# Layer norm and two-matmul MLP on one core: the third token tile loaded behind two weight pieces, its cells run later, and tile 3's chain rearranged

## The chip, the cores and the metric

The kernel runs on one core of a Trainium2 chip. A core has five engines with queues of their own: TensorE (PE, matmuls; its weight loads are listed as PEld), VectorE (DVE), ScalarE (ACT), GpSimd (POOL) and SyncE (SP, which here only issues transfers). Sixteen DMA engines carry the transfers. The metric is the device time of one execution in microseconds (us), as a median of several runs.

## The reference

```python
def reference(x, w1, b1, w2, b2):
    y = _layernorm(x, axis=-1)
    h = _gelu(jnp.einsum("bsd,df->bsf", y, w1) + b1)
    return jnp.einsum("bsf,fd->bsd", h, w2) + b2
```

x is 1 x 2048 x 1024, w1 is 1024 x 3584, w2 is 3584 x 1024, all bf16. The layer norm has no scale and no shift: (x - m) / sqrt(v + eps) for each token.

## The kernel before

The 2048 tokens are worked on in four blocks of 512, a block in four tiles of 128 tokens. Per block there are two matmul stages. The first (mm1) makes 28 rows r of 128 hidden channels: for each row, eight steps dt over the 1024 input channels, w1's piece as the weights and the transposed tokens (yT_sb) as the moving side, summed in one bank of PSUM (the accumulation memory, eight banks of 2 KB per partition). ACT reads the bank, applies gelu with the bias and writes hT_sb. The second (mm2) makes, for each of the four tiles, two halves of 512 output channels over 28 steps; DVE adds b2 (line 459) and SP stores.

Each of the five engines has a list of instructions in a fixed order, written out by hand for the start and, for DVE's later work, by a small planner (lines 631 to 646) from estimated times. Instructions wait on each other by semaphores; an engine that waits holds up all that is behind it in its list.

The change is in the start, block 0. There the transposed tokens are needed before the layer norm's statistics can be ready, so tiles 0, 1 and 2 (RAW) go through mm1 **raw**, unnormalised, and are corrected later:

- PE transposes a tile by eight matmuls against an identity (`pe_T`, line 335) into PSUM, one 128 x 128 block per input step dt. ACT copies the blocks into yT_sb (line 351). GROUPS_0 = (0, 4, 8) says that tiles 0 and 1 leave in two copies of four blocks; tile 2, by GROUPS_2 = (0, 2, 8), in two and six. Four banks take the groups: tile 0 in "t" and "2_0", tile 1 in "2_1" and "1_4", and tile 2 again in "t" and "2_0", so its transposes wait until ACT has read tile 0's.
- The **wave** is the first eight rows of mm1 (one bank each) on the three raw tiles. One matmul of it, one row r with one step dt, is a cell here (`wave_cell`, `pe_wave`, line 396). Its moving side is 128 columns per tile, with two columns of ones ahead of tile 0 that give the column sums of the weights.
- w1's first eight rows come in nine pieces, loads "w0" to "w8", in the order of PIECES: w0 holds dt 0 of rows 0 to 3, w1 (the load) dt 1, w2 dt 2 and 3, w3 dt 4 and 5, w4 dt 6 and 7, and w5 to w8 the same for rows 4 to 7, two steps each. (So "w0" to "w8" are pieces of the matrix w1.) w0 and w1 are 128 KB, the others, and a tile of x, 256 KB. SP issues them in the order of SP_FIRST_LOADS.
- For piece 0 the cells run for tiles 0 and 1 together (258 columns) and then for tile 2 (128); from piece 1 on, all three tiles at once (386).
- DVE takes the statistics (bn_stats, line 247, bn_aggr, line 257), POOL the power -0.5 (line 254). The means and the reciprocal deviations of the raw tiles are turned from columns into rows by DVE (`ops_row_turn`, line 479: turn_m for the means, turn_r for the deviations, four instructions each) and spread to all partitions by ACT (`put_row_spread`, line 485).
- **Tile 3** is normalised on DVE (line 261), transposed there within blocks of 32 (xq, line 489), and its sixteen pieces are moved into place by DVE (`moves_3`, line 494, those in DVE_MOVES) and ACT (`put_moves_3`, line 503, the rest). Its cells (line 396, 128 columns) follow the wave.
- DVE then corrects each bank of the wave (`ops_fix`, lines 532 and 535) and subtracts the means in yT_sb (`ops_centre`, line 525) for the rows of block 0 that follow; these are scaled at line 422.

DVE's order in the start is one line (542):

```python
seq = st[0] + st[1] + st[2] + turn_m + st[3] + turn_r[:3] + nm[3] + moves_3() + turn_r[3:] + ctr[:2]
```

and PE's order is that of the calls from line 546 on:

```python
pe_T(0, GROUPS_0, ("t", "2_0"))
pe_T(1, GROUPS_0, ("2_1", "1_4"))
pe_T(2, GROUPS_2, ("t", "2_0"))
```

with the wave's cells behind them.

Of the kernel before, what the change touches and what calls it, by code (L numbers as in the profile page):

```python
# [9 lines left out]
I32 = mybir.dt.int32  # L10

LN_EPS = 1e-5
P = 128
TB = 512
TPB = TB // P
# [4 lines left out]
TAIL_PIECES = (448, 64)  # L20
RAW = (0, 1, 2)
N_WARM = 25
GROUPS_0 = (0, 4, 8)
GROUPS_2 = (0, 2, 8)
HALVES = (0, 4, 8)
PIECES = ((0, 1, (0, 1, 2, 3)), (1, 2, (0, 1, 2, 3)), (2, 4, (0, 1, 2, 3)), (4, 6, (0, 1, 2, 3)), (6, 8, (0, 1, 2, 3)),
          (0, 2, (4, 5, 6, 7)), (2, 4, (4, 5, 6, 7)), (4, 6, (4, 5, 6, 7)), (6, 8, (4, 5, 6, 7)))
CENTRE = (0, 2, 4, 6, 8)
DVE_MOVES = ((0, 0), (1, 1), (2, 2), (3, 3), (0, 1), (1, 2), (2, 3))
W1_COLS = (512, 1024, 1024)  # L30
N_W2_CHUNKS = 4
SP_FIRST_LOADS = ("b1", "x0", "x1", "x2", "w0", "w1", "w2", "w3", "x3", "w4", "w5", "w6", "w7", "w8")
N_ONES = 2
PAD = 64

# [56 lines left out]
def bass_standalone__mixer_channel_mlp__prompt_kernel(  # L92
# [13 lines left out]
    DT = D // P  # L106
# [7 lines left out]
    R = R_WAVE  # L114
    assert R == NB1 + NB2 + 1 and R < FT
    assert NB1 + NB2 + 1 <= 8 and NB2 == 2
    assert all(c[-1] == DT for c in (GROUPS_0, GROUPS_2, HALVES))
    assert TPB == 4 and RAW == (0, 1, 2)
# [23 lines left out]
    with ExitStack() as es:  # L142
# [6 lines left out]
        yT_sb = sb("yT_sb", [P, 2, DT, PAD + TB], BF16)  # L149
# [26 lines left out]
        act = _Prog("s_act")  # L176
# [34 lines left out]
        def issue(item):  # L211
            if item == "b1":
                dma_q[0] = act
                dma(b1r_sb[:, :], b1.rearrange("(t p) -> t p", p=P), "b1", F * 2)
                dma_q[0] = sp
            elif item[0] == "x":
                load_x_tile(int(item[1:]))
            elif item[0] == "w" and int(item[1:]) < len(w1_chunks):
                load_w1(int(item[1:]))

        act.op(lambda e: e.preload_act_table(ACT.Gelu_apprx_tanh))
        for item in SP_FIRST_LOADS:
            issue(item)
# [8 lines left out]
        for b in range(2, NB):  # L232
# [4 lines left out]
                sig="ident")  # L237
# [7 lines left out]
        def op_stats(i, h):  # L245
            pw = D // parts(i)
            return (lambda e, i=i, h=h, pw=pw: e.bn_stats(st_sb[i][:, 6 * h:6 * (h + 1)],  # L247
                                                          x_sb[:, i, h * pw:(h + 1) * pw]),
                    [x_ev[i][h if len(x_ev[i]) == parts(i) else 0]], f"st{i}_{h}", 0.03 + pw * 0.0012)
# [41 lines left out]
        ybuf = lambda b: (b + 1) % 2  # L291
# [16 lines left out]
        def dve_put(o):  # L308
            dve.op(o[0], waits=o[1], sig=o[2])

        pe_t = [T_PE_START]
        bank_read = {}
        bank_of = {"t": ps_t[:, 0, :], "2_0": ps_2b[:, 0, :], "2_1": ps_2b[:, 1, :], "1_1": ps_1b[:, 1, :], "1_2": ps_1b[:, 2, :], "1_3": ps_1b[:, 3, :],
                   "1_4": ps_1b[:, 4, :]}
        ycol = lambda i: PAD + (i % TPB) * P
        raw_at = TB - len(RAW) * P
        one0 = raw_at - N_ONES

        def pe_T(i, groups, banks):
            blk = i // TPB  # L320
            src_ev = y_ev[i] if i in y_ev else [x_ev[i][0]] * DT
            evs = yT_ev.setdefault(i, [None] * DT)
            prev = None
            for k, (g0, g1) in enumerate(zip(groups[:-1], groups[1:])):
                bname = banks[k]
                for j in range(g0, g1):
                    waits = []
                    if bname != prev:
                        waits = ["ident"] + ([bank_read[bname]] if bname in bank_read else [])
                        off = 0  # L330
                    prev = bname
                    if j == g0 or src_ev[j] != src_ev[j - 1]:
                        waits.append(src_ev[j])
                    last = j == g1 - 1 and (k + 1 == len(banks) or banks[k + 1] != bname)
                    pe.op(lambda e, i=i, j=j, o=off, bap=bank_of[bname]: e.transpose(  # L335
                        out=bap[:, o:o + P], in_=x_sb[:, i, j * P:(j + 1) * P], identity=ident[:, :]),
                        waits=waits, sig=(f"tp{i}_{k}" if last else None))
                    evs[j] = f"te{i}_{k}"
                    off += P
            off = 0  # L340
            prev = None
            for k, (g0, g1) in enumerate(zip(groups[:-1], groups[1:])):
                bname = banks[k]
                if bname != prev:
                    off = 0
                prev = bname
                done = max(m for m in range(len(banks)) if banks[m] == bname)
                src = bank_of[bname][:, off:off + (g1 - g0) * P].bitcast(I32)
                src = src.rearrange("p (j s) -> p j s", j=g1 - g0)
                dst = yT_sb[:, 0 if i in RAW else ybuf(blk), g0:g1, ycol(i):ycol(i) + P].bitcast(I32)  # L350
                act.op(lambda e, dst=dst, src=src: e.copy(out=dst, in_=src), waits=[f"tp{i}_{done}"],  # L351
                       sig=f"te{i}_{k}")
                off += (g1 - g0) * P
                bank_read[bname] = f"te{i}_{k}"
            pe_t[0] += DT * 0.056

        unit_n = [0]
        bank_gelu = {}
# [124 lines left out]
        def put_row_spread(k, q0, q1):  # L483
            for q in range(q0, q1):
                act.op(lambda e, q=q: e.copy(out=row_b(k)[32 * q:32 * (q + 1)], in_=row_b(k)[0:32]),  # L485
                       waits=[f"row_q{k}"], sig=(f"row_{k}" if q == 3 else None))

        def moves_3():
            res = [(lambda e: e.transpose(out=xq_sb[:, :], in_=x_sb[:, 3, :]), [y_ev[3][-1]], "xq", 1.07)]
            for n, (tq, q) in enumerate([(tq, q) for tq in range(4) for q in range(4)]):  # L490
                src = xq_sb[32 * tq:32 * (tq + 1), :].rearrange("p (j q s) -> p j q s", j=DT, q=4)[:, :, q, :].bitcast(I32)
                dst = yT_sb[32 * q:32 * (q + 1), ybuf(0), :, ycol(3) + 32 * tq:ycol(3) + 32 * (tq + 1)].bitcast(I32)
                if (tq, q) in DVE_MOVES:
                    res.append((lambda e, src=src, dst=dst: e.tensor_copy(out=dst, in_=src), ["xq"],
                                ("tc3" if len(res) == len(DVE_MOVES) else None), 0.2))
            return res

        def put_moves_3():
            todo = [(tq, q) for tq in range(4) for q in range(4) if (tq, q) not in DVE_MOVES]
            for tq, q in todo:  # L500
                src = xq_sb[32 * tq:32 * (tq + 1), :].rearrange("p (j q s) -> p j q s", j=DT, q=4)[:, :, q, :].bitcast(I32)
                dst = yT_sb[32 * q:32 * (q + 1), ybuf(0), :, ycol(3) + 32 * tq:ycol(3) + 32 * (tq + 1)].bitcast(I32)
                act.op(lambda e, src=src, dst=dst: e.copy(out=dst, in_=src), waits=["xq"],
                       sig=("te3" if (tq, q) == todo[-1] else None))
            yT_ev[3] = ["te3"] * DT
# [32 lines left out]
        st = {i: [op_stats(i, 0), op_stats(i, 1), op_aggr(i)] for i in range(TPB)}  # L538
        nm = {3: ops_norm(3)}
        turn_m, turn_r = ops_row_turn(0), ops_row_turn(1)  # L540
        ctr = ops_centre()
        seq = st[0] + st[1] + st[2] + turn_m + st[3] + turn_r[:3] + nm[3] + moves_3() + turn_r[3:] + ctr[:2]
        for o in seq:
            dve_put(o)

        pe_b1()
        put_b1()
        pe_T(0, GROUPS_0, ("t", "2_0"))
        pe_T(1, GROUPS_0, ("2_1", "1_4"))
        pe_T(2, GROUPS_2, ("t", "2_0"))  # L550
        put_row_spread(0, 1, 4)
        wave = [new_unit() for _ in range(R)]
        opened = set()

        def wave_cell(r, dt, tiles, sig=None):
            waits = [] if r in opened else wave[r][1]
            opened.add(r)
            pe_wave(r, dt, tiles, wave[r][0], waits, sig)

        first = [(r, dt) for r in PIECES[0][2] for dt in range(*PIECES[0][:2])]  # L560
        for tiles in (RAW[:2], RAW[2:]):
            for r, dt in first:
                wave_cell(r, dt, tiles)
        cells = [(r, dt) for j0, j1, rows in PIECES[1:] for r in rows if r < R for dt in range(j0, j1)]
        for n, (r, dt) in enumerate(cells):
            wave_cell(r, dt, RAW, f"raw_{r}" if dt == DT - 1 else None)
        cs_ev = {}
# [34 lines left out]
        for b in range(NB):  # L602
            if b + 1 < NB:
                tiles = list(range((b + 1) * TPB, (b + 2) * TPB))
# [9 lines left out]
            for st in range(TPB):  # L614
                for dh in range(DH):
                    c0, c1 = dh * NCH, (dh + 1) * NCH
                    ob = (b * TPB + st) % NOB
                    prev = store_last.get((ob, dh))
# [14 lines left out]
        while ci < len(crit) or fi < len(fill):  # L633
            take_crit = fi >= len(fill)
            if not take_crit and ci < len(crit):
                rel_f, _, blk_f = fill[fi]
                if crit[ci][0] <= max(t_dve, rel_f) + CRIT_SLACK and blk_f > crit[ci][2]:
                    take_crit = True
            if take_crit:
                rdy, o, _ = crit[ci]  # L640
                ci += 1
            else:
                rdy, o, _ = fill[fi]
# [46 lines left out]
```

## Time and profile before

| | |
|---|---|
| time, median of 3 runs | 396.66 us (396.55 to 396.83) |
| the profiled execution | 396.68 us, of which the span, from the first to the last instruction, 395.3 us |
| mm1's matmuls (line 381, both banks' rows) | 152.4 and 31.9 us busy |
| mm2's matmuls (line 448) | 193.3 us busy |
| the start's cells (line 396, ps) | 13.1 us busy |
| ACT's gelu (line 406) | 64.0 and 12.4 us busy |
| DVE's transposes of the later blocks (line 303) | 83.7 us busy |
| HBM read, written | 19.14 MB, 4.19 MB |

In the views a row has the start and the length in us (in a timeline), or the busy time and the mean length in ns (in the groups), then the engine, the line of the kernel, the operation, what it writes <- what it reads, and the shapes. A bracket says how long the engine stood idle before the row and what released it. Rows of one kind that follow each other are merged, with their number behind the x; the length is then from the first one's start to the last one's end. The length of a PE row includes the time that a matmul needs to run through the array, so queued matmuls overlap: it is the distance between starts that says how fast they go. Transfers have the time from issue to landing.

### The profile page before, as it was taken

To read this page: it belongs to the slowest core of one execution; us is meant where nothing else is said; L and a number is where in the kernel's file an instruction comes from. 1 tells how busy PE (TensorE), PEld (TensorE's weight loads), DVE (VectorE), ACT (ScalarE), POOL (GpSimd) and SP (SyncE) were. 2 spreads that over 40 slices of the span, in tenths; PEclk is the share of its full clock that TensorE was granted. 3 is DMA by queue.
4 is the path that set the end of the run, shared out by engine and by line. 5 is a ranking of instruction groups with operands and counts; after the bars stand their busy time and mean duration, and the time that the engine had idled before them with its cause. 6 is when DMAs were issued, how large, how long until landed. Compare 5 with 4: busy or idle time off the path is not lost.

```text
span 395.3 us, 4518 instructions
## 1 busy us (share of the span) xinstructions
PE 390.3 (99%) x1904; PEld 184.5 (47%) x1938; DVE 162.8 (41%) x342; ACT 85.9 (22%) x139; POOL 10.5 (3%) x55
## 2 busy tenths in 40 slices
PE   8999999999999999999999999999999999999998
PEld 6744444444444444444444444444444444444444
DVE  6998889998999306987100000011100000001011
ACT  4655420000134332000023443000003334400000
POOL 3001000011001100000000000000000000000000
DMA  8999930000000000000000000000000000000000
GB/s 272 372 386 387 387 141 27 15 27 14 28 0 0 2 0 0 29 26 13 28 13 0 2 0 2 13 13 28 25 14 15 0 0 2 0 15 27 13 28 27
DMA packets 16077, 23.62 MB, mean 60 GB/s; under 512 B 1082, under 2 KB 8250, under 8 KB 16058
## 3 DMA queue, kind: packets, MB, share of 16 engines
q1 hardware_dynamic: 16016, 23.33, 16.7%
q8 instruction: 15, 0.25, 0.3%
q14 instruction: 4, 0.03, 0.0%
q10 hardware_dynamic: 42, 0.01, 0.0%
HBM read 19.14 MB, written 4.19 MB: 59 GB/s over the span
## 4 chain that ended last, share of the span: by engine, by line
PE 99%; issue 0%; ACT 0%; DVE 0%
PE ps L448 49%; PE ps L381 38%; PE ps_t L381 7%; PE ps L396 3%; PE ps L470 1%; PE ps_t L396 0%; ACT yT_sb L351 0%; PE ps_t L335 0%; PE ps L335 0%; DVE o_sb L459 0%; PE ps L508 0%
## 5 line engine op out<-in xcount | busy, mean ns | idle before, releaser
L448 PE MATMUL ps<-w_sb,hT_sb 128*128 128x512 bf16 (+2 forms) x909 | 193.3, 372 | 0.8
L381 PE MATMUL ps<-yT_sb,w_sb 128*128 128x512 bf16 x678 | 152.4, 379 | 0.9
L448 PEld LDWEIGHTS ps<-w_sb,hT_sb 128*128 128x128 bf16 x924 | 88.6, 98 | 105.2
L406 ACT ACTIVATE hT_sb<-ps,b_sb 128x512 bf16<-128x512 f32 x94 | 64.0, 687 | 234.7 <-PE ps L381 217.2
L381 PEld LDWEIGHTS ps<-yT_sb,w_sb 128*128 128x128 bf16 x696 | 68.1, 98 | 81.9
L459 DVE TENSOR_TENSOR o_sb<-ps,b_sb 128x512 bf16<-128x512 f32 (+2 forms) x33 | 22.3, 676 | 198.7 <-PE ps L448 198.5
L303 DVE STREAM_TRANSPOSE yT_sb<-x_sb 32x256 bf16<-32x256 bf16 x192 | 83.7, 436 | 21.9 <-PE ps_t L381 18.8
L381 PE MATMUL ps_t<-yT_sb,w_sb 128*128 128x512 bf16 x135 | 31.9, 379 | 0.1
L247 DVE BATCH_NORM_STATS2 st_sb<-x_sb 128x6 f32<-128x512 bf16 x32 | 21.0, 672 | 3.6 <-DMA x_sb<-in_x_dram 3.5
L381 PEld LDWEIGHTS ps_t<-yT_sb,w_sb 128*128 128x128 bf16 x136 | 13.3, 98 | 16.0
L406 ACT ACTIVATE hT_sb<-ps_t,b_sb 128x512 bf16<-128x512 f32 x18 | 12.4, 687 | 17.1 <-PE ps_t L381 14.6
L396 PE MATMUL ps<-yT_sb,w_sb 128*128 128x128 bf16 (+2 forms) x116 | 13.1, 269 | 0.0
L396 PEld LDWEIGHTS ps<-yT_sb,w_sb 128*128 128x128 bf16 x116 | 8.9, 98 | 3.5
L422 DVE TENSOR_TENSOR ps<-ps,row_r 128x384 f32<-128x384 f32 x17 | 9.2, 563 | 3.1 <-PE ps L381 2.8
L254 POOL TENSOR_TENSOR rstd_sb<-mv_sb,nhalf 128x1 f32<-128x1 f32 x13 | 7.1, 548 | 116.7 <-DVE mv_sb L257 116.7
L261 DVE TENSOR_SCALAR x_sb<-x_sb,mv_sb,rstd_sb 128x1024 bf16<-128x1024 bf16 x13 | 7.0, 541 | 1.9 <-POOL rstd_sb L254 1.3
L532 DVE SCALAR_TENSOR_TENSOR ps<-row_r,ncs,ps 128x384 f32<-128x384 f32 x7 | 4.2, 614 | 0.4 <-PE ps L396 0.4
L535 DVE TENSOR_TENSOR ps<-ps,row_r 128x384 f32<-128x384 f32 x7 | 3.9, 563 | 0.2
L525 DVE TENSOR_TENSOR yT_sb<-yT_sb,row_r 128x768 bf16<-128x768 bf16 x4 | 3.6, 952 | 0.0
L470 PE MATMUL ps<-const-bfloat16-1.0 128*128 128x128 bf16 x25 | 2.8, 309 | 0.8 <-PEq L675 0.8
L485 ACT COPY row_r<-row_r 32x384 f32<-32x384 f32 x6 | 3.1, 510 | 2.2 <-DVE row_r L479 2.1
L257 DVE BATCH_NORM_AGGREGATE mv_sb<-st_sb 128x2 f32<-128x15 f32 x13 | 2.9, 222 | 0.4
(33 smaller groups left out, 31.1 us busy)
## 6 DMA issues: line engine op xcount, KB each, us to landing
w_sb<-in_w_dram SPq DMA_DIRECT2D x4, 1792.0 KB, 18.3
w_sb<-in_w_dram SPq DMA_DIRECT2D x2, 2048.0 KB, 16.2
out_dram<-o_sb SPq DMA_DIRECT2D x31, 128.0 KB, 1.7
x_sb<-in_x_dram SPq DMA_DIRECT2D x3, 1024.0 KB, 14.4
w_sb<-in_w_dram SPq DMA_DIRECT2D x7, 256.0 KB, 4.9
x_sb<-in_x_dram SPq DMA_DIRECT2D x4, 256.0 KB, 3.4
w_sb<-in_w_dram SPq DMA_DIRECT2D x1, 1024.0 KB, 9.5
w_sb<-in_w_dram SPq DMA_DIRECT2D x2, 128.0 KB, 3.8
```

The lines of the kernel that those rows point to most:

```text
L247: return (lambda e, i=i, h=h, pw=pw: e.bn_stats(st_sb[i][:, 6 * h:6 * (h + 1)], x_sb[:, i, h * pw:(h + 1) * pw]), [x_ev[i][h if len(x_ev[i ...
L254: pool.op(lambda e, i=i, dst=dst, mv=mv: e.tensor_tensor(out=dst, in0=mv[:, 1:2], in1=nhalf[:, i:i + 1], op=ALU.pow), waits=[f"mv{i}", "nh ...
L261: return (lambda e, i=i, c0=c0, c1=c1: e.tensor_scalar(out=x_sb[:, i, c0:c1], in0=x_sb[:, i, c0:c1], scalar1=mv_sb[:, i, 0:1], scalar2=rst ...
L303: res.append((lambda e, src=src, dst=dst: e.transpose(out=dst, in_=src), waits, (f"tr{i}" if lastop else None), 0.47))
L381: pe.op(lambda e, b=b, r=r, dt=dt, bank=bank: e.matmul(unit_bank(bank)[:, 0:TB], lhsT=w1_sb[:, dt, r * P:(r + 1) * P], rhs=yT_sb[:, ybuf(b ...
L396: pe.op(lambda e: e.matmul(unit_bank(bank)[:, n0:n1], lhsT=w1_sb[:, dt, r * P:(r + 1) * P], rhs=yT_sb[:, 0 if tiles[0] in RAW else ybuf(0) ...
L406: act.op(lambda e, r=r, n0=n0, n1=n1, bank=bank: e.activation(out=hT_sb[:, r, n0:n1], in_=unit_bank(bank)[:, n0:n1], func=ACT.Gelu_apprx_tanh,
L422: crit.append((est[sig], (lambda e, reg=reg: e.tensor_tensor(out=reg, in0=reg, in1=row_b(1), op=ALU.mult), [sig, "row_1"], ready, 0.57), 0))
L448: pe.op(lambda e, sl=sl, ft=ft, c0=c0, c1=c1, bank=bank: e.matmul(ps_2[:, bank, 0:c1 - c0], lhsT=hT_sb[:, ft, sl * P:(sl + 1) * P], rhs=w2 ...
L459: crit.append((est[sig], (lambda e, ob=ob, c0=c0, c1=c1, bank=bank: e.tensor_tensor(out=o_sb[:, ob, c0:c1], in0=ps_2[:, bank, 0:c1 - c0], ...
L470: pe.op(lambda e: e.matmul(ps_1[:, 0, 0:P], lhsT=ones, rhs=ones, start=True, stop=True))
L532: return [(lambda e: e.scalar_tensor_tensor(out=reg, in0=row_b(0), scalar=ncs[:, c:c + 1], in1=reg, op0=ALU.mult, op1=ALU.add), [f"m1_0_{r ...
```

## The change

- SP's order of first loads puts x2 behind w0 and w1.
- GROUPS_0 becomes (0, 2, 8): tiles 0 and 1 leave PSUM in copies of two and six blocks. The copies, which `pe_T` put on ACT's list itself, get a function of their own, `put_copy`, and go in turn: tile 0's two blocks, tile 1's two blocks, tile 0's six, tile 1's six.
- The transposes of tile 2 and ACT's spread of the row of means are put behind the cells of pieces 0 and 1 for tiles 0 and 1. Piece 0's cells run for tile 0 and then for tile 1 alone; pieces 1 and 2 for tiles 0 and 1 together; tile 2's cells of pieces 0, 1 and 2 follow piece 2. From piece 3 on all three tiles run together as before.
- DVE does two of the four turns of the means before the statistics of tile 3 and two behind them; all four turns of the deviations go behind tile 3's moves. DVE does five of the sixteen moves, not seven; ACT eleven, not nine.

```diff
-GROUPS_0 = (0, 4, 8)
+GROUPS_0 = (0, 2, 8)
...
-DVE_MOVES = ((0, 0), (1, 1), (2, 2), (3, 3), (0, 1), (1, 2), (2, 3))
+DVE_MOVES = ((0, 0), (1, 1), (2, 2), (3, 3), (0, 1))
...
-SP_FIRST_LOADS = ("b1", "x0", "x1", "x2", "w0", "w1", "w2", "w3", "x3", "w4", "w5", "w6", "w7", "w8")
+N_EARLY = 2
+N_PAIR = 3
+SP_FIRST_LOADS = ("b1", "x0", "x1", "w0", "w1", "x2", "w2", "w3", "x3", "w4", "w5", "w6", "w7", "w8")
...
-        def pe_T(i, groups, banks):
+        def pe_T(i, groups, banks, copies=True):
...
+            pe_t[0] += DT * 0.056
+            for k in (range(len(banks)) if copies else ()):
+                put_copy(i, groups, banks, k)
+
+        def put_copy(i, groups, banks, k):
+            g0, g1 = groups[k:k + 2]
+            bname = banks[k]
...
+            act.op(lambda e, dst=dst, src=src: e.copy(out=dst, in_=src), waits=[f"tp{i}_{done}"],
+                   sig=f"te{i}_{k}")
+            bank_read[bname] = f"te{i}_{k}"
...
-        seq = st[0] + st[1] + st[2] + turn_m + st[3] + turn_r[:3] + nm[3] + moves_3() + turn_r[3:] + ctr[:2]
+        seq = st[0] + st[1] + st[2] + turn_m[:2] + st[3] + turn_m[2:] + nm[3] + moves_3() + turn_r + ctr[:2]
...
-        pe_T(0, GROUPS_0, ("t", "2_0"))
-        pe_T(1, GROUPS_0, ("2_1", "1_4"))
-        pe_T(2, GROUPS_2, ("t", "2_0"))
-        put_row_spread(0, 1, 4)
+        pe_T(0, GROUPS_0, ("t", "2_0"), False)
+        pe_T(1, GROUPS_0, ("2_1", "1_4"), False)
+        for k in range(2):
+            put_copy(0, GROUPS_0, ("t", "2_0"), k)
+            put_copy(1, GROUPS_0, ("2_1", "1_4"), k)
...
-        first = [(r, dt) for r in PIECES[0][2] for dt in range(*PIECES[0][:2])]
-        for tiles in (RAW[:2], RAW[2:]):
-            for r, dt in first:
-                wave_cell(r, dt, tiles)
-        cells = [(r, dt) for j0, j1, rows in PIECES[1:] for r in rows if r < R for dt in range(j0, j1)]
+        cells_of = lambda a, b: [(r, dt) for j0, j1, rows in PIECES[a:b] for r in rows for dt in range(j0, j1)]
+        for t in RAW[:2]:
+            for r, dt in cells_of(0, 1):
+                wave_cell(r, dt, (t,))
+        for r, dt in cells_of(1, N_EARLY):
+            wave_cell(r, dt, RAW[:2])
+        pe_T(2, GROUPS_2, ("t", "2_0"))
+        put_row_spread(0, 1, 4)
+        for r, dt in cells_of(N_EARLY, N_PAIR):
+            wave_cell(r, dt, RAW[:2])
+        for r, dt in cells_of(0, N_PAIR):
+            wave_cell(r, dt, RAW[2:])
+        cells = cells_of(N_PAIR, len(PIECES))
```

More of the change, by code (lines that the diff above doesn't have):

```diff
@@ L339, in pe_T @@
                     off += P
-            off = 0
[L341 to L355, printed above, removed]
+            pe_t[0] += DT * 0.056
[4 more added lines that the diff above has]
+            bname = banks[k]
+            assert banks.count(bname) == 1
+            off = 0
+            done = max(m for m in range(len(banks)) if banks[m] == bname)
+            src = bank_of[bname][:, off:off + (g1 - g0) * P].bitcast(I32)
+            src = src.rearrange("p (j s) -> p j s", j=g1 - g0)
+            dst = yT_sb[:, 0 if i in RAW else ybuf(i // TPB), g0:g1, ycol(i):ycol(i) + P].bitcast(I32)
+            act.op(lambda e, dst=dst, src=src: e.copy(out=dst, in_=src), waits=[f"tp{i}_{done}"],
+                   sig=f"te{i}_{k}")
+            bank_read[bname] = f"te{i}_{k}"
         unit_n = [0]
```

## The prediction

> **What bounds the kernel now.** I read the page first, then the chain of waits, then the timelines of PE and ACT over the first 25 us, then the landings of the first loads.
>
> ```profile
> span 395.3 us, 4518 instructions
> ...
> PE 390.3 (99%) x1904; PEld 184.5 (47%) x1938; DVE 162.8 (41%) x342; ACT 85.9 (22%) x139; POOL 10.5 (3%) x55
> ...
> PE 99%; issue 0%; ACT 0%; DVE 0%
> ```
>
> TensorE (PE) is the bound in all stages. So the change can only win where PE stands still, or by giving PE less to do. The timeline of PE from 4.98 us on shows the only place:
>
> ```profile
> 4.82 0.39 PE L335 MATMUL ps<-ident,x_sb 128*128 128x128 bf16 x4
> 5.78 0.27 PE L335 MATMUL ps_t<-ident,x_sb 128*128 128x128 bf16 x2 [0.58 <-ACT yT_sb L351]
> 5.89 0.50 PE L335 MATMUL ps<-ident,x_sb 128*128 128x128 bf16 x6
> 6.22 0.99 PE L396 MATMUL ps<-yT_sb,w_sb 128*128 128x258 bf16 x9
> ```
>
> The first line's four transposes start 0.056 us apart, so the array has taken the last at 4.82 + 4 x 0.056 = 5.04. Nothing starts until 5.78: **0.74 us of idle**. The view charges it to an ACT copy, but that copy was over at 4.73; the last to come is x2. Its transfer was issued at 1.69 and took 4.0 us, so it landed at 5.64, and PE's first transpose starts 0.14 after that. From 5.78 on matmul follows matmul at the pitch of its width (0.056 us for 128 columns, 0.110 for 258, 0.164 for 386, 0.216 for 512) up to 393.3. The single holes of 0.216 us, one per 50 matmuls, are missing records: the next matmul starts exactly two pitches later.
>
> **Ceiling.** The change splits 16 cells (a cell is one weight load with its matmul) in two: 4 of 258 columns, 12 of 386. The widths add up the same, and 2 x 0.056 - 0.110 and 0.110 + 0.056 - 0.164 are both 0.002 to 0.003, so this costs 16 x 0.0026 = 0.04 us. If all idle goes, the gain is 0.74 - 0.04 = 0.70 us, or 0.18%.
>
> **Loads.** SP issues one load every 0.47 us, whatever its order. From 2.5 us on the profile by stretches has the DMA engines full (share 0.85 to 1.16, 260 to 401 GB/s), so the order decides who waits, not the sum. A load counts as landed when the slowest of 16 engines has landed. In the trace, median engine and slowest:
>
> x0 3.37 and 3.50; x1 4.02 and 4.13; x2 4.67 and 5.64; w0 5.10 and 6.03; w1 5.50 and 6.37; w2 6.29 and 7.07; w3 7.05 and 7.74; x3 7.86 and 8.46.
>
> One engine falls 0.97 behind during x2 and stays 0.6 to 0.9 behind; over the eleven loads from x2 to w8 its middle lag is 0.70. After the change w0 and w1 (128 KB each) take the place of x2 (256 KB). By medians: w0 4.02 + 0.43 = 4.45, w1 4.85, x2 5.5, and **w2 as now, 6.27, since the same bytes lie ahead of it**. Slowest engine with 0.70 of lag: w0 about 5.2, w1 5.5, x2 6.2, w2 6.97. Landings without lag (0.11, as at x1): w0 4.6, w1 5.0, x2 5.6, w2 6.4. I take the lag, since nine loads in a row carry it and neither order nor size changed it; both ends stay for the range.
>
> **Copies.** These ACT rows price them:
>
> ```profile
> 4.36 0.37 ACT L351 COPY yT_sb<-ps_t 128x256 int32<-128x256 int32 x1 [0.36 <-PE ps_t L335]
> 4.78 0.92 ACT L351 COPY yT_sb<-ps 128x256 int32<-128x256 int32 x3
> 6.09 0.27 ACT L351 COPY yT_sb<-ps_t 128x128 int32<-128x128 int32 x1 [0.38 <-PE ps_t L335]
> 6.42 0.48 ACT L351 COPY yT_sb<-ps 128x384 int32<-128x384 int32 x1
> ```
>
> Four blocks take 0.37, two 0.27, six 0.48; queued copies start 0.067 per block apart (three of four blocks in 0.92). Tile 0's first two transposes end at 4.11, and a copy starts 0.04 after: 4.15 to 4.41, against 4.36 to 4.73 now. Tile 1's first two end at 4.87: 4.90 to 5.17. The six-block copies queue behind: 5.04 to 5.52, 5.44 to 5.92 (now all done by 5.71). The last is needed by PE only for the third piece, so 0.21 later costs nothing unless that piece starts before 5.95. Tile 0's second copy is ready at 4.78 and waits in ACT behind tile 1's first until 5.04; PE's transposes of x2 need its bank, at 5.52, still ahead of x2's landing.
>
> **PE after, step by step.** Transposes of tiles 0 and 1 end at 5.04, as now. Four cells of tile 0 wait for w0 (5.2, plus 0.14 from landing to matmul): 5.34 to 5.57; tile 1, 0.22, to 5.79; second piece, 4 x 0.110, to 6.23 (w1 is there). Transposes of tile 2 wait for x2 at 6.2: 6.34 + 8 x 0.056 = 6.79. Now the third piece: **it waits for w2, 6.97 + 0.14 = 7.11**. Eight cells of 0.110 to 7.99, then the sixteen held-back cells of tile 2 at 0.056, to 8.88. Before, the same work (first pieces of all three tiles) ended at 6.89 + 12 x 0.164 = 8.85. So +0.03 us. What went wrong with the idea, if this holds: w2 had 7.54 - 7.07 = 0.47 us of slack, because tile 2's cells ran before it; with these moved behind w2 the slack is gone and the old idle turns into waits for w0, x2 and w2. With x2 at its lagged 6.37 and w2 at 7.07, as in the profiled execution, it is 7.21 + 1.78 = 8.99, or +0.14. Behind it w3 (7.74 against 8.88) and all later pieces have time.
>
> **Tile 3's chain and the row turns.**
>
> ```profile
> 13.16 1.61 DVE L494 COPY yT_sb<-xq_sb 32x128 int32<-32x128 int32 x7
> 13.16 2.75 ACT L503 COPY yT_sb<-xq_sb 32x128 int32<-32x128 int32 x9 [1.25 <-DVE xq_sb L489]
> ...
> 16.69 3.29 PE L396 MATMUL ps<-yT_sb,w_sb 128*128 128x128 bf16 x56
> ...
> 17.34 1.15 DVE L532 SCALAR_TENSOR_TENSOR ps<-row_r,ncs,ps 128x384 f32<-128x384 f32 x2 [0.41 <-PE ps L396]
> ```
>
> Two row turns (0.28 each) go behind st[3]: it starts at 8.47 (x3 lands 8.46), not 9.03, so everything to xq comes 0.56 earlier and two turns (0.56) go in while POOL makes rstd: norm at 10.74 instead of 11.30, xq over at 12.57 instead of 13.13. DVE copies five (0.23 apart) instead of seven, ACT eleven (0.31 apart) instead of nine: ACT ends at 12.60 + 11 x 0.31 = 16.0, against 15.91. ACT's row spread (1.55) now starts at 10.5, not 9.03, and ends at 12.05, before xq. All four turns of the second row follow (1.1), then the two subtractions (1.83): DVE is free at about 16.8, against 16.93. PE reaches tile 3's cells at 16.85 now and its copies end at 15.91: 0.94 of slack, still 0.85. DVE's fixes wait 0.41 for PE. Worth **nothing** now; if PE came 0.66 earlier it would still hold. The cover is gone if PE comes over 0.8 earlier, which the ceiling excludes. ACT's bank releases behind it keep their place (the tightest, ps_t, is released at 28.60 and used at 28.89), since fixes and cells move together.
>
> **Sum.** +0.03 us on the profiled 396.68 us (span 395.3 and 1.4 around it), 0.02 from the median 396.66: **396.7 us**.
>
> **A rule against it.** Matmuls start 0.107 us apart up to 4.64 and 0.056 after, and the one idle of 0.74 behind this did not bring the slow pitch back. The Trainium skill, "TensorE: Matmul & The Clock Gate", section "A second HAM failure mode: psum-queue depth-cycling", says that short, frequent idling between groups of matmuls can make the clock swing between half and full. By that, three short waits in place of one would be worse than their sum; no run so far shows it.
>
> **Rivals.**
> - *The lag does not come.* It began in x2, which now flows elsewhere. w2 at 6.4: T0 and T1 cells from 5.04, second piece to 5.92, transposes to 6.37, third piece from 6.54, end at 8.3 or, with w2 a bit sooner, 8.2: -0.55 to -0.66, so **396.05**. For: at x1 all engines are within 0.27. Against: the lag stays in every load after x2, and the four times of before lie within 0.28 us, so it is no rare event. Between this and the forecast the gain falls 1:1 with w2's landing.
> - *A longer lag.* The turn from x rows to weight rows now comes twice. From 6.94 on each us of w2 costs one us. At the greatest lag shown (0.97) w2 is at 7.24: +0.3, **397.0**. To lose over 0.79 it must land after 7.73, a lag of 1.46, which no load shows.
> - *The clock falls back* in the new waits. It decides once the waits make PE's share of a few us too small. Slow pitch lasted 3.8 us at the start; the same again does 1.9 us of work less, of which up to 0.7 falls in waits anyway: +1.2 to +1.9, **398.3**.
>
> **Chances.** A measurement here tells about 0.2% (0.79 us) from no change. Forecast (w2 6.75 to 7.2, 396.45 to 396.95) 0.52; lag smaller or gone (396.0 to 396.45) 0.26; longer lag (to 397.45) 0.08; beyond that 0.04; clock 0.06; a gain beyond the ceiling, if runs idle more than the profiled one, 0.04. Faster 0.04, same 0.86, slower 0.10. From 396.05 to 397.1 I leave out about 0.2.
>
> **What would show it.** PE's stretch from 5.04 to the fourth piece: waits at the first cell, the first transpose of tile 2 and the first cell of the third piece, each 0.14 behind a landing; the last one's end near 8.9. Wrong if w2 lands before 6.75 or after 7.25, if cells run at the 0.107 pitch after 5 us, or if PE waits at 16.85 for tile 3.

## The result and the profile after

The changed kernel takes 397.38 us (median of 14 runs, 396.83 to 398.73), the kernel before 396.53 in the same comparison (14 runs, 396.13 to 396.91): a ratio of 1.0023, 95% interval 1.0015 to 1.0032. It is **slower by 0.85 us**, a small loss, but the whole interval lies above 1; 396.7 was predicted. The profiled execution took 397.58 with a span of 396.2, 0.9 more than before's.

The page of the changed kernel still has PE as the bound; new is the DMA in the chain that ended last.

```profile
span 396.2 us, 4582 instructions
...
PE 98%; DMA 1%; SPq 0%; issue 0%; DVE 0%
```

Its timeline of PE from 5 to 10 us (start, length, line, operation, what it writes and reads):

```profile
4.75 0.79 PE L337 MATMUL ps<-ident,x_sb 128*128 128x128 bf16 x6
5.38 0.61 PE L398 MATMUL ps<-yT_sb,w_sb 128*128 128x130 bf16 x8
6.24 0.61 PE L398 MATMUL ps<-yT_sb,w_sb 128*128 128x258 bf16 x4 [0.24 <-DMA w_sb<-in_w_dram]
7.25 0.28 PE L337 MATMUL ps_t<-ident,x_sb 128*128 128x128 bf16 x2 [0.40 <-DMA x_sb<-in_x_dram]
7.38 0.50 PE L337 MATMUL ps<-ident,x_sb 128*128 128x128 bf16 x6
8.00 2.26 PE L398 MATMUL ps<-yT_sb,w_sb 128*128 128x258 bf16 x26
```

The one idle ahead of tile 2 has become three waits: for w1 (0.41 us between the array's work, from the distances of starts), for x2 (0.57) and for w2 (0.29). The first cells ran at 5.38, right behind the transposes, since w0 was there, but the fourth piece (steps 4 and 5) starts at 9.77, where before it started at 8.85. That is +0.92, the whole difference of the spans; tile 3's first cell still comes 0.92 later (17.61 against 16.69). The waits sum to 1.27 us against 0.74; the rest is mainly PE's slow pitch, which held the transposes until 5.38, not 5.04.

What moved is the landings. w2's transfer, issued at 3.1 us in both kernels, took 4.0 us before and 4.8 after (the last number of each row, before first):

```profile
w_sb<-in_w_dram SPq DMA_DIRECT2D x1, 256.0 KB, 4.0
```

```profile
w_sb<-in_w_dram SPq DMA_DIRECT2D x1, 256.0 KB, 4.8
```

The stretches from 4 to 6 us, after and then before (the last two columns are the DMA engines' share and GB/s):

```profile
4.00:4.50 0.50, 0.50 (x7) 0.50 (x6) 0.50 (x2) 0.27 (x1) 0.00 (x0) 1.00 1.20 158
4.50:5.00 0.50, 0.50 (x8) 0.50 (x6) 0.47 (x3) 0.01 (x1) 0.00 (x0) 1.00 0.54 141
5.00:5.50 0.50, 0.50 (x9) 0.50 (x8) 0.50 (x2) 0.50 (x2) 0.44 (x1) 1.00 0.95 217
5.50:6.00 0.50, 0.49 (x9) 0.32 (x6) 0.50 (x2) 0.50 (x2) 0.11 (x1) 1.00 0.76 225
```

```profile
4.00:4.50 0.50, 0.50 (x8) 0.50 (x6) 0.50 (x2) 0.14 (x1) 0.00 (x0) 1.00 1.08 338
4.50:5.00 0.50, 0.50 (x11) 0.50 (x8) 0.47 (x3) 0.45 (x2) 0.00 (x0) 1.00 0.85 260
5.00:5.50 0.50, 0.20 (x4) 0.03 (x1) 0.50 (x2) 0.50 (x3) 0.35 (x1) 1.00 1.03 352
5.50:6.00 0.50, 0.22 (x4) 0.25 (x5) 0.50 (x2) 0.21 (x1) 0.20 (x1) 1.00 1.08 356
```

For two microseconds the engines move 141 to 225 GB/s instead of 260 to 356, though their share of busy time is mostly high. Most packets still take 0.05 us (1 KB) or 0.08 us (2 KB), but sixteen that start between 4.1 and 5.8 us take 0.45 to 1.37 us. This is called the stall below. Median engine and slowest: w0 4.30 and 4.41, w1 4.70 and **6.19**, x2 6.21 and **7.21**, w2 7.00 and **7.87**.

### The profile page after: what moved, and what is told of

The parts are those of the page before. It is cut to its first block, busy times and chain, and to the rows that moved or that the text cites. A ratio compares the mean times of both kernels' runs of the same rounds, so it can differ in the third digit from the quotient of the medians.

```text
span 396.2 us, 4582 instructions
## 1 busy us (share of the span) xinstructions
PE 392.8 (99%) x1954; PEld 185.5 (47%) x1954; DVE 161.9 (41%) x340; ACT 86.7 (22%) x141; POOL 10.4 (3%) x55
## 4 chain that ended last, share of the span: by engine, by line
PE 98%; DMA 1%; SPq 0%; issue 0%; DVE 0%
PE ps L450 49%; PE ps L383 38%; PE ps_t L383 7%; PE ps L398 3%; DMA x_sb<-in_x_dram 1%; PE ps_t L398 0%; SPq L190 0%; PE ps L337 0%; PE ps_t L337 0%; DVE o_sb L461 0%
## 5 line engine op out<-in xcount | busy, mean ns | idle before, releaser
L398 PE MATMUL ps<-yT_sb,w_sb 128*128 128x128 bf16 (+3 forms) x132 | 13.5, 257 | 0.4 <-DMA w_sb<-in_w_dram 0.2
L505 ACT COPY yT_sb<-xq_sb 32x128 int32<-32x128 int32 x11 | 3.2, 295 | 0.3 <-DVE xq_sb L491 0.2
```

What stands on the lines that cost most here:

```text
L398: pe.op(lambda e: e.matmul(unit_bank(bank)[:, n0:n1], lhsT=w1_sb[:, dt, r * P:(r + 1) * P], rhs=yT_sb[:, 0 if tiles[0] in RAW else ybuf(0) ...
```

## The experiments

The table has what decides for most kernels: third load that SP issues, landing of the load with steps 2 and 3 (w2) by median and slowest engine, start of PE's piece of steps 4 and 5 ("4th piece"), time against the kernel before of the same comparison, with the interval of the ratio. Landings and starts are from one trace each. e8, e10 and e11 differ in what lies ahead of w2 or in when it is issued; they are told below.

| kernel | third load | w2 median, slowest | 4th piece | median time, before's | ratio (95%) |
|---|---|---|---|---|---|
| before | x2 | 6.29, 7.07 | 8.85 | 396.53 | |
| e12, before again | x2 | 6.34, 6.73 | 8.57 | 396.41 (one) | |
| after | w0 | 7.00, 7.87 | 9.77 | 397.38, 396.53 | 1.0015 to 1.0032 |
| e13, after again | w0 | 7.00, 7.67 | 9.57 | 397.40 (one) | |
| e1, order only | w0 | 6.46, 7.55 | 11.80 | 397.84, 396.71 | 1.0021 to 1.0055 |
| e2, old order | x2 | 6.27, 6.56 | 8.69 | 396.77, 396.71 | 0.9993 to 1.0019 |
| e3, old tile 3 | w0 | 6.71, 8.18 | 10.08 | 397.44, 396.71 | 1.0001 to 1.0022 |
| e4, x2 in halves | w0 | 6.75, 7.58 | 9.49 | 397.45, 396.71 | 1.0006 to 1.0029 |
| e5, x2 from w1 | w0 | 6.64, 7.58 | 9.49 | 397.23, 396.58 | 1.0009 to 1.0027 |
| e6, w0 and w1 from x | w0 | 6.91, 7.66 | 9.56 | 397.04, 396.58 | 1.0003 to 1.0021 |
| e9, merged | w0 (256 KB) | 6.47, 7.43 | 9.37 | 397.07, 396.61 | 1.0003 to 1.0020 |
| e15, contiguous | w0 | 6.21, 7.90 | 9.80 | 397.26, 396.68 | 1.0004 to 1.0026 |
| e14, far x2 | x2 | 6.22, 6.72 | 8.61 | 396.55, 396.68 | 0.9985 to 1.0004 |
| e16, third from w1 | x2 | 6.41, 7.69 | 9.13 | 396.62, 396.54 | 0.9993 to 1.0012 |
| e17, third in 1 KB | x2, half | 6.78, 6.95 | 9.39 | 397.10, 396.54 | 1.0006 to 1.0025 |

**The parts.**

```diff
-SP_FIRST_LOADS = ("b1", "x0", "x1", "x2", "w0", "w1", "w2", ...
+SP_FIRST_LOADS = ("b1", "x0", "x1", "w0", "w1", "x2", "w2", ...   # e1, on the kernel before
```

> The kernel before with one edit: x2 is issued behind w0 and w1. Theory L (loads): in the trace of the changed kernel x2's and w1's packets take 0.4 to 1.4 us instead of 0.05 to 0.09 from 4.2 us on, w1 lands at 6.2 and x2 at 7.2, and every later load is 0.6 to 0.8 late, because x rows follow weight rows on the engines. Then it comes here too: x2 lands at 7.0 to 7.3, all cells wait behind tile 2's transposes, and the first cell starts near 7.8 instead of 6.22: +1.2 to +1.6 us. Rival C (compute): the stall is chance or comes at 4 to 5 us in any order, and the loss is made by the moved cells; then x2 lands at about 6.4 and the first cell starts at 6.95: +0.7 us.

The order alone costs 1.13 us in the median, no less than the whole change (the two intervals overlap, so "more" is not shown): x2 landed at 6.92, its transposes ran at 7.06 and the first cell at 7.50. That is nearer to theory L than to C, a little short of L's range. A second cost came with it in the execution that was profiled. PE's timeline, then two stretches of PE's time (PEclk is the third column from the end):

```profile
4.33 0.67 PE L335 MATMUL ps<-ident,x_sb 128*128 128x128 bf16 x9
7.06 0.27 PE L335 MATMUL ps_t<-ident,x_sb 128*128 128x128 bf16 x2 [2.07 <-DMA x_sb<-in_x_dram]
```

```profile
7.10:11.10 4.00, 4.00 (x24) 2.57 (x25) 3.83 (x10) 2.15 (x5) 0.55 (x1) 0.57 0.95 318
11.20:15.20 4.00, 4.00 (x26) 2.39 (x25) 3.81 (x13) 0.49 (x4) 0.55 (x1) 1.00 1.10 364
```

By starts PE stood idle for 2.2 us. From 7.1 to 11.1 us the granted clock was 0.57 in the mean, and up to 10.9 cells of 386 columns started 0.32 us apart, not 0.164. This is the profiled execution, at 399.61 us; three of the twelve (399.60 to 399.68) have such a mean clock, 0.996 over the whole, the others 1.0, so it explains these three and not the median. The clock rival of the prediction thus exists, in this kernel, with a longer idle than the change makes.

e2 is the changed kernel with the old order:

```diff
-SP_FIRST_LOADS = ("b1", "x0", "x1", "w0", "w1", "x2", "w2", ...
+SP_FIRST_LOADS = ("b1", "x0", "x1", "x2", "w0", "w1", "w2", ...
```

> The changed kernel with the old order of loads (x2 ahead of w0 and w1); all the rest of the change stays. Theory L: landings as before (x2 5.6, w0 6.0, w1 6.4, w2 7.1, none later than 0.2 from that). PE waits for w0 until 6.17, then 0.45 for piece 0, 0.44 for piece 1, 0.45 for tile 2's transposes, 0.88 and 0.90 for piece 2 and tile 2's cells: end 9.29 against 8.85, +0.4 us, less than the change's +0.85, and its times scatter less. Rival C: the moved cells carry the loss, so it stays at +0.8 us or more.

The compute side alone is worth nothing that can be measured: +0.06 us, where +0.4 was expected (the interval, up to +0.75, doesn't exclude it). PE's timeline has no wait behind the first cell, which came when w0 had landed (the bracket names a copy of ACT's that was over before):

```profile
5.58 1.05 PE L398 MATMUL ps<-yT_sb,w_sb 128*128 128x130 bf16 x12 [0.41 <-ACT yT_sb L355]
6.47 0.28 PE L337 MATMUL ps_t<-ident,x_sb 128*128 128x128 bf16 x2
6.58 0.50 PE L337 MATMUL ps<-ident,x_sb 128*128 128x128 bf16 x6
6.92 2.26 PE L398 MATMUL ps<-yT_sb,w_sb 128*128 128x258 bf16 x26
```

Here w0's slowest landed at 5.45, not 6.03, so the cells began at 5.58 and the fourth piece at 8.69; by the expectation's own terms (its five parts sum to 3.12) 5.58 + 3.12 = 8.70. e1 and e2 together put the loss on the order of loads. e3 puts DVE's order and moves back in the changed kernel:

```diff
-seq = ... turn_m[:2] + st[3] + turn_m[2:] + nm[3] + moves_3() + turn_r + ctr[:2]
+seq = ... turn_m + st[3] + turn_r[:3] + nm[3] + moves_3() + turn_r[3:] + ctr[:2]
```

> The changed kernel with DVE's old order (four turns of the means ahead of tile 3's statistics, three turns of the deviations ahead of its norm) and seven moves on DVE, nine on ACT. Theory L: this part lies beside PE's work and is worth nothing: the time is the changed kernel's, 397.2 to 397.6 us (+0.7 to +0.9). Rival D (the DVE and ACT part of the change costs): 0.3 us or more less than the changed kernel.

It stays at the changed kernel's time (397.44): this part is off the path. In the changed kernel itself:

```profile
13.43 3.36 ACT L505 COPY yT_sb<-xq_sb 32x128 int32<-32x128 int32 x11 [0.16 <-DVE xq_sb L491]
```

```profile
18.26 1.15 DVE L534 SCALAR_TENSOR_TENSOR ps<-row_r,ncs,ps 128x384 f32<-128x384 f32 x2 [0.69 <-PE ps L398]
```

ACT's copies of tile 3 end at 16.79 and PE comes for them at 17.61: 0.82 us of slack. DVE waits 0.69 for PE.

**What the stall is not.** In e4 x2 comes as two loads of 512 columns with 1 KB packets.

```diff
...
+for h in range(2):   # where i == 2
+    dma(x_sb[:, i, h * HC:(h + 1) * HC], xf[i * P:(i + 1) * P, h * HC:(h + 1) * HC], f"x{i}_{h}", P * HC * 2)
...
```

> The changed kernel with x2 loaded as two transfers of 512 columns, so that its packets are 1 KB like those of the weight pieces beside it; the transposes and statistics wait for the half they need. If the stall comes from the change of packet size (2 KB behind 1 KB), the packets take 0.05 to 0.1 us, the second half lands before 6.5 and w2 near 7.1: 396.4 to 396.9 us. If it comes from going from w1's place in memory to x's and back, the stall stays, and so does +0.6 to +0.9 us.

The stall stays (packets of 0.41 to 1.05 us that start at 4.25 to 5.25), so it isn't the step from 1 KB to 2 KB packets. Next theory: the turn of the stream from x's memory to w1's and back.

```diff
+src = w1[0:P, D:2 * D] if i == 2 else xf[i * P:(i + 1) * P, :]   # e5
+src = xf[(4 + ci) * P:(5 + ci) * P, 0:b - a].unsqueeze(1) if ci < 2 else w1v[:, j0:j1, a:b]   # e6
```

> The changed kernel, but x2's load reads 128 rows of 2 KB of the weight matrix w1 (its columns 1024 to 2047) instead of tile 2 of x, so tile 2 is computed on other data; destination, sizes and order are unchanged. Theory T (turns): an engine's packets stall when the stream goes from x's memory to w1's or back while others are still in the first; the change has two more turns, and this kernel takes these two away. Then w2's median engine lands at 6.2 to 6.4 and its slowest before 6.8, and the time is 0.5 to 0.9 us below the changed kernel's, 396.4 to 396.9 us. Rival P (place): what stalls is the early, strided weight pieces or the time of 4 to 5 us, whatever x2 reads: w2's slowest stays at 7.5 to 8.2 and the time at 397.2 to 397.6 us.

> The counterpart: the changed kernel, but the loads of w0 and w1 read 128 rows of 1 KB of x (tiles 4 and 5) instead of their pieces of w1, so steps 0 and 1 of rows 0 to 3 are computed on other weights. Five loads from x, then weights: the two extra turns are gone too. Theory T: no long packets before 5 us, w1 and x2 with all engines within 0.3 us of the median, w2 after the one turn at a median of 6.2 to 6.4; 0.5 to 0.9 us below the changed kernel. Rival P: since the early pieces now are not w1's rows, it also lands well; but if only their 1 KB packets matter, it stalls as before at 4.2 us.

Both keep the stall, e6 with packets of 0.54 to 0.70 us that start at 3.8 to 5.1 us, by their place in the queue all in loads from x. That theory fell. e8 moves x2 behind w3:

```diff
+SP_FIRST_LOADS = ("b1", "x0", "x1", "w0", "w1", "w2", "w3", "x2", "x3", "w4", ...
+N_EARLY = 4
+N_PAIR = 4
```

> The changed kernel with x2 moved on behind w3, directly ahead of x3, and the pieces 0 to 3 run for tiles 0 and 1 before tile 2's transposes (N_EARLY and N_PAIR 4). The turns between x and w1 are as many as in the kernel before (three), not five. Theory T: w0 lands at 4.4, w1 at 4.8, w2 at 5.6, w3 at 6.4, each within 0.2 of its median, x2 with the turn's stall at 7.2 to 8.0; PE runs from 5.1 with little idle until tile 2's transposes. Its time then hangs on tile 3's chain, since the statistics of tile 2 wait for x2 (1 us later on DVE): 396.2 to 397.5 us. Rival P: long packets at 4.2 to 5 us in the early pieces here too, w2 slowest after 6.5.

w1 landed at 5.63 and w2 at 7.69, though no x tile lies between them and w2 has 256 KB less ahead of it, so an x tile between weight pieces is not the trigger. PE stood 1.69 us for w2; the time, 398.37 against 396.58 (five runs, 1.0031 to 1.0058), lies above the 397.5 that was expected as the most. Then size, packets and time:

```diff
+PIECES = ((0, 2, (0, 1, 2, 3)), (2, 4, (0, 1, 2, 3)), ...   # e9: w0 and w1 as one load
...
+b = R * P if ci < 2 else b   # e10: steps 0 and 1 for eight rows, 2 KB packets
...
+dma(..., ["eps9"] if i == 0 else [])   # e11: the first load waits for a memset
```

> The changed kernel with its first two weight pieces of 128 KB as one load of 256 KB (two 1 KB packets per partition), so that every load after b1 is 256 KB and x2 is SP's fourth load of that size; its cells of steps 0 and 1 run for tile 0, then for tile 1, and x2's transposes follow. Theory S (small loads): two loads of 128 KB early in the queue leave the engines with too little queued behind them, some engines run dry or wait while others go on. Then here no long packets at 4 to 5 us, w0 lands by 5.0, x2 by 5.8, the next piece (steps 2 and 3) by 6.6, the fourth piece's cells start near 8.3, and the time is 396.0 to 396.4 us. Rival P (1 KB packets ahead of the fourth or fifth microsecond stall in any size of load): the slowest engine of steps 2 and 3 stays at 7.4 to 8.2, and the time at 397.0 to 397.6 us.

> The changed kernel with steps 0 and 1 loaded for all eight rows at once: 128 rows of 2 KB (256 KB) each, in the order x0, x1, w0, x2, w1, w2; the later load of steps 0 and 1 for rows 4 to 7 falls away, and w1's cells run behind tile 2's transposes. All packets up to w1 are 2 KB. Rival P (the 1 KB packets of the early weight pieces stall): no packet over 0.3 us before 6 us, w0 lands by 4.9, x2 by 5.6, w1 by 6.3; w2, 256 KB later than in the changed kernel, by 7.1; time 396.3 to 396.9 us. Theory F (something at a fixed time, 3.8 to 5 us, stalls whatever flows): long packets there all the same, w2 at 7.8 or later, 397.2 to 398 us.

> The changed kernel with SP's first load held back until a memset of POOL's at about 1.9 us has run, so that all loads come about 1.1 us later against the engines' work. Theory F (fixed time): the long packets stay at 4.2 to 5 us, and now fall in x1's and w0's packets. Rivals S and P (tied to the stream): they move to 5.3 to 6.1 us and fall in w1's and x2's packets again. The time is the changed kernel's plus about 1 us and says nothing more.

e9 stalls with loads of 256 KB (packets of 0.3 to 1.0 us from 3.5 on), so theory S falls. e10 stalls with 2 KB packets (one of 1.02 at 3.53; w2, which has 256 KB more ahead, at 7.97; 397.59 against 396.61, 1.0014 to 1.0032), so P falls. In e11, run once, the loads are issued 1.2 us later, and the first long packets of the weights come at 5.47 instead of 4.18: the stall goes with the stream, not with the time (398.43 us, span 397.0). Twelve of x0's packets, at 3.0 to 3.3, are long there too (0.45 to 0.57); no theory here says why.

> The kernel before once more, for a second trace. If the 0.97 us by which one engine lagged in x2 is a habit of this order, w0's slowest engine lands at 5.9 to 6.1 again and PE's idle ahead of tile 2 is 0.7 us; if it is chance, w0 may land at 5.3 to 5.6 and the idle be 0.2 to 0.5.

> The changed kernel once more, for a second trace. If the stall belongs to this order, w2's slowest engine is again at 7.5 to 8.2 us and PE waits at the same three places; if the first trace was a bad draw, w2 is at 7.1 or earlier and the sum of the waits under 0.8 us.

The landings of both kernels repeat in their kind: w2's slowest at 6.73 and 7.67. The changed kernel's waits repeat only in part: e13 waits for x2 (0.39) and w2 (0.57), not for w1. Before's lag of 0.97 in x2 does not repeat: it is 0.20 in e12, and there is no idle ahead of tile 2, since x2 was there at 4.91 and PE's slow pitch held the transposes until 5.4.

**Where the rows lie.**

```diff
+at = 12 if i == 2 else i   # e14, on the kernel before: x2 reads tile 12
+at = 3 if i == 2 else i   # e15: x2 reads tile 3
...
+src = xf[h0:h0 + P // 2, :].rearrange("r (h c) -> (r h) c", h=2).unsqueeze(1)   # e15: w0, w1 read on where x1 ended
```

> The kernel before, its order of loads too, but x2's load reads tile 12's rows of x instead of tile 2's, so the third load doesn't go on where the second ended in memory; tile 2 is computed on other data. Theory M (memory): engines stall where the stream leaves a run of neighbouring rows, in whatever load comes third. Then this kernel stalls as the changed one does: packets over 0.4 us at 3.5 to 4.5 us, x2's slowest engine 0.8 or more behind the median, w2's slowest at 7.3 or later, and 0.4 to 1.0 us more than the kernel before. Rival Q (the queue): three loads of x first are harmless for another reason, the rows' place doesn't matter: w2's slowest lands by 7.1 and the time is the kernel before's, within 0.2 us.

> The changed kernel, but w0, w1 and x2 read on in x where x1 ended: w0 and w1 128 pieces of 1 KB each from rows 256 to 383, x2 rows 384 to 511, so that the first five loads are one run of neighbouring bytes; steps 0 and 1 of rows 0 to 3 are computed on other weights and tile 2 on tile 3's data. Theory M: no packet over 0.3 us before the turn to w2; w1's slowest engine lands by 5.1, x2's by 5.8, w2's by 7.0; the time is 396.2 to 396.8 us. Rival Q: it stalls as the changed kernel does (w1's slowest at 5.6 or later, w2's at 7.5 or later), 397.0 to 397.6 us.

e14 is harmless, and e15 helps only up to w1 (slowest 4.95); then a packet of 1.36 us starts at 4.83, and x2's slowest engine lands at 7.11. Neighbouring rows are not it. Last, one property of the third load at a time, in the kernel before:

```diff
+src = w1[0:P, D:2 * D] if i == 2 else xf[i * P:(i + 1) * P, :]   # e16; e17 has e4's two halves
```

> The kernel before, order and compute unchanged, but x2's load reads 128 rows of 2 KB of w1 instead of tile 2, which is then computed on other data. If a third load from another matrix than the first two starts the stall (theory T2, a weaker form of the theory of turns: only the first turn counts, and the later it comes the less it costs), w2's slowest lands at 7.3 or later, w0's at 6.0 or later, and the time is 0.3 to 1 us more than the kernel before's. If the third load only has to have 2 KB packets (theory K), w2's slowest is at 6.5 to 7.1 and the time is the kernel before's within 0.2 us.

> The kernel before, but x2 is loaded as two transfers of 512 columns with 1 KB packets; its data and the order are the same, SP issues one load more and so the weights 0.47 us later. Theory K (1 KB packets in the third load start the stall): packets over 0.5 us near 4.2, w2's slowest at 7.5 or later, time 0.3 to 1 us more than the kernel before's. Theory T2: the third load still comes from x, no stall: w2's slowest at 6.6 to 7.2, time within 0.2 us of the kernel before's.

On the landings T2 fits both: e16 stalls (packets of 0.4 to 0.75 us at 3.5 to 4.3; w2 at 7.69, as late as in the changed kernel), and in e17 w2 lands well (6.95, with one issue more ahead). On the times K fits both, +0.08 and +0.56 us. So neither holds whole; e6 and e15, whose third load reads x too and whose w2 is late, speak against T2 as well. In e17 the cost is not K's stall: PE waits 0.26 us for the load behind w2, which landed at 9.34.

e16 costs nothing measurable, 1.0003: there tile 2's cells run ahead of w2's. In its trace, which is of one of its two slowest runs, PE stands 0.13 us for w2 at 7.69 (its matmuls start at 7.53 and 7.82, elsewhere 0.164 apart). The view names no DMA, but w2's first weight load starts 0.10 behind the landing:

```profile
7.79 0.29 PEld L397 LDWEIGHTS ps<-yT_sb,w_sb 128*128 128x128 bf16 x3 [0.32 <-issue]
```

e16 thus shows the other half of the cause: **a w2 as late as the changed kernel's makes PE wait 0.13 us in the old order of cells; in the new one each us of its lateness counts whole.**

## Why the prediction was wrong

- **The step that failed** is "w2 as now, 6.27, since the same bytes lie ahead of it", with the slowest engine at 6.97. It was 7.87 and 7.67 in two traces, 0.7 to 0.9 later, and the median engine was late as well (7.00). Equal bytes behind equal issue times are not an equal landing: the engines moved less than 60% of the rate for two microseconds (185 against 327 GB/s from 4 to 6 us). The rate was taken from the old order's stretches and carried over.
- **The arithmetic behind it held.** Landing + 0.14 + 0.88 + 0.90 gives 7.87 + 1.92 = 9.79 (9.77 measured) and 7.67 + 1.92 = 9.59 (9.57 in e13). PE started on w1 and on x2 only 0.05 behind their landings, not 0.14. The slack of 0.47 us that w2 loses was named, and e16 shows it at work.
- **The rival "a longer lag"** had the right price (1:1 from 6.94 on) and too small a size. In the changed kernel w2's own lag, 0.87 and 0.67, stayed under the bound of 0.97; what moved is its median, 0.73 later than 6.27, which the rival held fixed. In e15 and e16 it is the lag instead, 1.7 and 1.3. "1.46, which no load shows" came true in w1 at once (4.70 to 6.19). One trace of one order can't bound another order's lag.
- **"The lag does not come"** came in none of the kernels that put a weight piece third.
- **The ceiling** of 0.70 us rested on one execution: the idle of 0.74 came from a lag and a pitch that the second trace, e12, doesn't repeat. How many runs have it is not known.
- **Tile 3's chain** was right in its outcome, worth nothing. That its slack measured 0.82 against 0.85 is partly luck: the prediction let PE reach these cells at 16.85 in the kernel before, where its own row says 16.69, so the working gives 0.69; and in the run both ends moved, PE by 0.92 and ACT's last copy to 16.79 instead of 16.0, since x3 landed 0.79 later.
- **ACT's copies**: the first of two blocks started at 4.14 (4.15 worked out). The rest started at 5.00 and ended at 6.06 (4.90 and 5.92 worked out), behind transposes at the slow pitch; the third piece, which needs them, started at 8.00.
- **The clock** did not fall back in the traces of the changed kernel; its pitch is 0.110 for 258 columns from 6.24 on. It fell in e1. PE's slow pitch lasted to 5.4 us instead of 4.6, but PE waited for w1 until 6.2 anyway.

What stays open is why engines stall here. The matrix, the packet size, the load's size, the rows' place and the time were each taken away alone without taking the stall away. All traces with w2 by 7.1 have a load from x into x_sb in third place (before, e12, e2, e14, and e17 with 1 KB packets); all others have it at 7.43 or later, e16 (from w1 into x_sb) and e15 (from x into w1_sb) among them. With one or two traces of each, that is an observation and no cause. Long packets come in the good orders too: the kernel before has two of 0.51 us ahead of 4.5 us and six of 0.4 to 0.8 from 6.4 us on, and in e12 and e2 w4 and x3 have engines 1.2 and 1.3 us behind the median. In these three traces PE does not wait for these loads. Open as well are two of the changed kernel's fourteen runs, at 398.7 us with a full clock, of which there is no trace.

## What to carry to other kernels

A load that is moved up is paid for by whoever loses its slack: before cells are put behind a landing, take that landing's lateness from several traces, and by its slowest engine. A rate that the queue reached in one order of loads is no price for another order; one run with only the order changed (here e1) would have shown the loss before the cells were rearranged.

## What the runs showed of the hardware

- The last of one transfer's sixteen engines can land 1.5 us behind the median (w1 in the changed kernel: median 4.70, last 6.19; PE starts on it at 6.24). The Trainium skill, "DMA: Bandwidth & Descriptors", section "Why a DMA increments its semaphore by 16 and not by 1", says that the engines finish on their own and only the full count means that all has landed; the trace agrees, and the last engine is the one that sets PE.
- An idle of 2.2 us on PE (e1) was followed by a mean granted clock of 0.57 from 7.1 to 11.1 us. The Trainium skill, "TensorE: Matmul & The Clock Gate", section "Why this matters for your kernels", warns of idle gaps over about 3 us; here a shorter one did it, soon after PE's pitch had first halved (at 4.2 us).
- The time at which PE's pitch first halves differs between executions of the same kernel: 4.6 us in before and 5.6 in e12.
